# Output rows in step order, the verdict inside the order, QT moves on two queues, other homes for the raw weights

## The chip, the core and the metric

The kernel runs on one core of a Trainium2 chip. The metric is the device time of one execution in microseconds (us). TensorE is called PE, VectorE DVE, ScalarE ACT, GpSimd POOL and SyncE SP, as the profile calls them. SP and POOL each have a queue from which they issue DMA transfers in order.

## The reference

A gated linear recurrence over the sequence is followed by a two-layer network with a squared ReLU. There are B=4 batches, H=8 heads, S=768 steps, D=48 channels per head; 3072 tokens, a model width of 384 and a hidden width of 2048. q, k, v and the complex gate a are float32; the two weights w_in (384x2048) and w_out (2048x384) arrive as 64-bit floats.

```python
mag = np.sqrt(a_re * a_re + a_im * a_im)
scale = np.minimum(mag, 0.999) / (mag + 1e-06)
a_re_n, a_im_n = (a_re * scale, a_im * scale)
for t in range(S):
    ar, ai = (a_re_n[:, :, t, :, None], a_im_n[:, :, t, :, None])
    kv = np.einsum('bhd,bhe->bhde', k[:, :, t], v[:, :, t])
    S_re, S_im = (ar * S_re - ai * S_im + kv, ar * S_im + ai * S_re)
    y[:, :, t] = np.einsum('bhd,bhde->bhe', q[:, :, t], S_re)
x = y.transpose(0, 2, 1, 3).reshape(B * S, H * D)
h = np.maximum(x @ w_in, 0.0)
out = (h * h) @ w_out
```

## The kernel before

`fast_path` cuts the 3072 tokens into six units n = 0 to 5 of 512 tokens. For each unit it records the following steps.

- `load(n)` brings a, q and k into `aq` (SP, L814) and v into `vv[n % 2]` (POOL, 16 transfers, L828). A partition holds four consecutive steps.
- `chain(n)` normalises the gate, forms running products within each group of four steps (`inner`, L888 to L894), inverts them (L901 to L913), turns the totals through PE (L946), scans them on DVE and turns them back (L1092, L1097); the products with q and k follow (L1134 to L1150), and `gather` (L1181) moves the K tiles with POOL.
- `pairs(n)` takes the four head pairs in turn. `turn_pe` (units 0 and 1, on PE and ACT) or `turn` (units 2 to 5) makes the QT tile. `turn` transposes 32x32 blocks on DVE (L1217), and 12 moves (b = 0 to 3, j = 0 to 2, L1221) on SP place them. `score` (L1257, masked on DVE in L1260), `keep` (L1273) and `mix` (L1303, L1307) are matmuls. ACT copies the mixed tile from PSUM to `yt` (L1313), and SP moves it into `xT` (L1320). In `yt` and `xT` the 128 tokens of a chunk stand in the order (c, t), c being the place within a group of four steps.
- `dense(n, grp)` does the network for 256 tokens: 96 matmul rows on w1 (L1342; the profile lists two rows for each call), ReLU and Square on ACT (L1370, L1371), twice 32 rows on w2 (L1382), a copy to `ot` on ACT (L1386), and the output. Because of the order (c, t), the 128 rows of a chunk go out in four transfers of 32 rows by POOL (L1391).

The weights come in 16 pieces of 768 KB as raw 64-bit words (`fetch`, L750, POOL) into tiles that are not in use yet, their raw homes; `convert` turns a piece into float32 with one ACT step (L760) and three DVE steps (L763, L765, L769). The homes of the second weight's pieces are listed in `raw2`; a fetch marked early waits only for the first gate tiles. At the end `inspect` fetches each raw piece again and `look` (L784, L786 on DVE) tests the exponents. The `verdict` reduces all tests to one flag, which each engine loads (L1460) to decide by `tc.If` (L1461) whether a slower general path has to run. The closing barrier is at L1488.

Nearly all of this is recorded with `step` and `dma` as steps of a `Plan`. Each step has an engine, an estimated length, reads, writes and a rank. `Plan.order` is a list scheduler: it takes the engine that is free first, and on it the ready step with the lowest rank. The order that it finds is the order in which each engine gets its instructions, and from then on engines and queues work strictly in that order. Real waits come from the tiles that the instructions use. The verdict is not a step: it is issued after `plan.emit()`, so its matmul (L1408) stands behind all products.

Of the kernel before, what the change touches and what calls it, by code (L numbers as in the profile page):

```python
# [480 lines left out]
class Plan:  # L481
# [8 lines left out]
        self.wrote = {}  # L490
        self.read = {}

    def add(self, eng, dur, reads, writes, fn, rank, wire=None, group=None):

        n = len(self.steps)
        deps = set()
        for k in reads:
            deps.update(self.wrote.get(k, (None, ()))[1])
        for k in writes:
            tag, last, base = self.wrote.get(k, (None, [], []))  # L500
            if group is not None and tag == group:
                deps.update(base)
                last.append(n)
            else:
                base = list(last) + self.read.get(k, [])
                deps.update(base)
                self.wrote[k] = (group, [n], base)
                self.read[k] = []
        for k in reads:
            self.read.setdefault(k, []).append(n)  # L510
        deps.discard(n)
        self.steps.append((eng, dur, sorted(deps), fn, rank, wire))
        return n
# [63 lines left out]
def fast_path(ctx, tc, q, k, v, a_re, a_im, moe_w_in, moe_w_out, out, flag):  # L577
# [97 lines left out]
    dve.memset(ypair, 0.0)  # L675
    for t in txs:
        pool.memset(t, 0.0)
    pool.memset(txs[0].rearrange("p r (m k) -> p r m k", k=8)[:, 0, :, 0], 1.0)
    pool.memset(txs[1].rearrange("p r (m k) -> p r m k", k=4)[:, 0, :, 0], 1.0)

# [5 lines left out]
    def ts2(n):  # L686
        return n / 1920.0 + 0.18
# [1 line left out]
    def ac(n):  # L689
        return n / 1200.0 + 0.18  # L690

    def step(eng, dur, reads, writes, fn, rank, wire=None, group=None):
        return plan.add(eng, dur, reads, writes, fn, rank, wire, group)

    def dma(q, reads, writes, fn, rank, size, lat=1.8, group=None):
        step("SP" if q is sp else "POOL", 0.6 if q is sp else 0.55,
# [19 lines left out]
    def two(t):  # L716
# [8 lines left out]
            )  # L725
    raw1 = [(three(t), keys) for t, keys in raw1]
    raw1.append((xT[:, 1].bitcast(U32), [("xT", 1, m) for m in range(NM)]))
    raw2 = [w2slot(3), w2slot(2), w2slot(3), w2slot(2),
            (QT[2].bitcast(U32)[:, 0:2 * PW], [("QT", 2)]),
            (vv[1].bitcast(U32), [("v", 1)]),  # L730
            (QT[0].bitcast(U32)[:, 0:2 * PW], [("QT", 0)]),
            (QT[1].bitcast(U32)[:, 0:2 * PW], [("QT", 1)])]
    raw2 = [(two(t), keys) for t, keys in raw2]

    def piece(i):
# [35 lines left out]
    def inspect(i):  # L771
        z, s = i % 2, (i // 2) % 2
        src = piece(i)[0]
        n = piece(i)[4]
        t = ff[z].bitcast(U32)[:, s * Z:(s + 1) * Z]
        keys = [("f", z, 2 * s), ("f", z, 2 * s + 1)]
        rank = (LATE, i)
        dma(pool, [("xT", (NU - 1) % 2, NM - 1)], keys,
            lambda: pool.dma_start(out=t.rearrange("p (m f) -> p m f", m=n), in_=src),
            rank, 2 * PW * 4 * C)  # L780
        hi = t.rearrange("p (n two) -> p n two", two=2)[:, :, 1]

        def look():
            dve.tensor_scalar(out=hi, in0=hi, scalar1=0x38000000, scalar2=0x78000000,  # L784
                              op0=ALU.bitwise_xor, op1=ALU.bitwise_and)
            dve.tensor_reduce(out=odd[:, i:i + 1], in_=hi, axis=AX, op=ALU.max)  # L786
        step("DVE", ts2(PW) + tt(PW), keys, keys + [("odd",)], look, rank)

# [10 lines left out]
    def load(n):  # L801
# [20 lines left out]
        for i in range(W):  # L822
            b, s = divmod(n * L + i * C, S)
            src = v[b, :, s:s + C, :].rearrange("h (t c) d -> c t h d", c=W)
            for c in range(W):
                vrank = rank if n else (CONV, 9)
                dma(pool, [("xT", n % 2, NM - 1)] if n else [("gate",)], [("v", n % 2)],
                    lambda i=i, c=c, src=src: pool.dma_start(  # L828
                        out=t[32 * c:32 * c + 32, i], in_=src[c]), vrank, 32 * 1536, 4.0,
                    group=n)  # L830

    def chain(n):
# [9 lines left out]

        def roots(z):
            f0, f1, m2, t = col[z]
            step("ACT", ac(Z), [("a", z)], key(z, 0, 1), lambda: act.activation(
                out=ff[z][:, 0:Z], in_=A[z], func=AF.Square,
                accum_out=sums[:, n, z:z + 1]), first)
            step("DVE", tt(Y), key(z, 0, 1), key(z, 2), lambda: dve.tensor_tensor(
# [15 lines left out]
        def normalise(z):  # L864
            f0, f1, _, t = col[z]
            step("ACT", ac(Y), key(z, 3), key(z, 0), lambda: act.activation(
                out=f0, in_=t, func=AF.Copy, scale=0.999), first)
            step("ACT", ac(Y), key(z, 3), key(z, 1), lambda: act.activation(
                out=f1, in_=t, func=AF.Copy, scale=-1e-6, bias=1.0), first)
            step("DVE", tt(Y), key(z, 0, 1), key(z, 0), lambda: dve.scalar_tensor_tensor(  # L870
                out=f0, in0=f0, scalar=1.0, in1=f1, op0=ALU.min, op1=ALU.mult), first)
            a2 = A[z].rearrange("p (r x) -> p r x", r=2)
            step("DVE", tt(Z), key(z, 0), [("a", z)], lambda: dve.tensor_tensor(  # L873
                out=a2, in0=a2, in1=f0.unsqueeze(1).to_broadcast([C, 2, Y]),
                op=ALU.mult), first)
            step("ACT", ac(Y), key(z, 3), [], lambda: act.activation(
                out=junk[:, 0:Y], in_=t, func=AF.Square, saturate=False,
                accum_out=sums[:, n, 2 + z:3 + z]), first)

# [76 lines left out]
        def totals(j):  # L956
# [31 lines left out]
            def scan_x():  # L988
# [18 lines left out]
                                          scalar1=2.0 ** 114, scalar2=None, op0=ALU.is_le)  # L1007
                if not ends:
                    dve.tensor_copy(out=cx, in_=x[:, :, C])
            step("DVE", 2.3, [b, ("cx",)], [("x",), ("cx",)], scan_x, rank)  # L1010

        def product(dst, xx, y, size, reads, writes):
            shape = list(xx.shape)
# [91 lines left out]
        vt = vv[n % 2]  # L1105
        for j in range(2):
            for r in range(2):
                step("ACT", ac(Y), [("qk", j)], [], lambda j=j, r=r: act.activation(
                    out=junk, in_=QK[j][:, ts(r, Y)], func=AF.Square, saturate=False,
                    accum_out=sums[:, n, 4 + 2 * j + r:5 + 2 * j + r]), rank)  # L1110
            step("ACT", ac(Y), [("v", n % 2)], [], lambda j=j: act.activation(
                out=junk, in_=vt[:, ts(j, Y)], func=AF.Square, saturate=False,
                accum_out=sums[:, n, 8 + j:9 + j]), rank)
        for j in (2, 0, 1):
# [80 lines left out]
    def pairs(n):  # L1195
# [9 lines left out]
        def turn(i):  # L1205
# [11 lines left out]
                     lambda nat=nat, dst=dst, j=j: dve.transpose(out=dst[:, j], in_=nat), rank)  # L1217
            for b in range(W):
                for j in range(NJ):
                    dma(sp, [("a", z) if i % 2 == 0 else ("qk", z)], [("QT", s)],  # L1220
                        lambda b=b, j=j, z=z, t=t, T6=T6: sp.dma_start(  # L1221
                            out=t[32 * j:32 * j + 32, b],
                            in_=T6[32 * b:32 * b + 32, i % 2, j]), rank, 65536,
                        group=(n, i))
# [70 lines left out]
        def mix(i):  # L1295
# [4 lines left out]
            def go():  # L1300
# [10 lines left out]
                 [("yp",)], go, rank)  # L1311
            y = take("yt", 2)
            step("ACT", ac(L), [("yp",)], [("yt", y)], lambda: act.copy(  # L1313
                out=yts[y][0:64 + D], in_=ypair[0:64 + D]), rank)
            for h in range(2):
                r, end = (2 * i + h) * D, (2 * i + h + 1) * D
                p = 64 * h
# [16 lines left out]
    def dense(n, grp):  # L1334
# [39 lines left out]
        for i in range(2):  # L1374
# [11 lines left out]
            step("ACT", ac(DM), [(b,)], [("ot", o)], lambda ps=ps, o=o: act.copy(  # L1386
                out=ots[o], in_=ps), (0, n))
            r = n * L + (2 * grp + i) * C
            dst = out[r:r + C, :].rearrange("(t c) e -> c t e", c=W)
            for c in range(W):  # L1390
                dma(pool, [("ot", o)], [], lambda c=c, o=o, dst=dst: pool.dma_start(  # L1391
                    out=dst[c], in_=ots[o][32 * c:32 * c + 32]), rank, 32 * DM * 4)

    def verdict():
        pool.memset(good, 1.0)
        for lo, hi, top_ in ((0, 2, 60), (2, 4, 12), (4, NS, 20)):
            dve.tensor_scalar(out=ok[:, :, lo:hi], in0=sums[:, :, lo:hi],
                              scalar1=2.0 ** top_, scalar2=None, op0=ALU.is_le)
        dve.tensor_reduce(out=good[:, 0:1], in_=ok, axis=AXY, op=ALU.min)
        dve.tensor_reduce(out=good[:, 1:2], in_=grow, axis=AXYZ, op=ALU.min)  # L1400
        dve.tensor_reduce(out=good[:, 2:3], in_=total, axis=AXY, op=ALU.min)
        dve.tensor_reduce(out=most, in_=odd, axis=AX, op=ALU.max)
        dve.tensor_scalar(out=good[:, 3:4], in0=most, scalar1=0.0, scalar2=None,
                          op0=ALU.is_equal)
        dve.tensor_reduce(out=good[:, 7:8], in_=good[:, 0:7], axis=AX, op=ALU.min)
        dve.memset(col, 1.0)
        ps = bank["tr0"][0:1, 0:1]
        pe.matmul(ps, lhsT=good[:, 7:8], rhs=col, start=True, stop=True)  # L1408
        dve.tensor_scalar(out=flag, in0=ps, scalar1=C - 0.5, scalar2=None, op0=ALU.is_lt)

    for n in range(NU):
        load(n)
# [4 lines left out]
                convert(i)  # L1417
        chain(n)
        if n == 0:
            for j in (0, 4, 5):  # L1420
                fetch(NPIECE + j)
        pairs(n)
        if n == 0:
            for j in (1, 6, 7):
                fetch(NPIECE + j, False)
            for j in (0, 1):
                convert(NPIECE + j)
            for j in (2, 3):
                fetch(NPIECE + j, False)
            for j in range(2, NPIECE):  # L1430
                convert(NPIECE + j)
        for grp in range(2):
            dense(n, grp)
    for i in range(2 * NPIECE):
        inspect(i)
    with tc.manual_schedule():
        plan.emit()
    verdict()


@with_exitstack
# [51 lines left out]
```

## Time and profile before

| | us |
|---|---|
| median of 3 runs | 749.65 (747.22 to 751.41) |
| profiled execution | 747.83 |
| its span, first to last instruction | 746.1 |
| busy: PE, DVE, ACT, POOL | 655.4, 510.8, 347.0, 209.9 |
| end of the last product on PE | 730.8 |

The page splits the span into 40 slices of 18.65 us; each digit is the busy share of a slice in tenths. A line of waits reads: engine, operation and line, what ended the wait, total us, times, longest us. A row of stretches reads: the stretch, its length, the busy us of PE, PE's weight loads, DVE, ACT and POOL with the instruction counts in brackets, then the granted clock of PE, the share of the DMA engines and GB/s. An engine's name with a q (SPq, POOLq, PEldq) is its sequencer.

### The profile page before, as it was taken

The page shows a single profiled execution, that of the slowest core. Times are in us where ns is not written, and L with a number is a line of the kernel's source. Part 1 is how long each engine was busy: PE and PEld are TensorE (multiplying, and loading weights), DVE is VectorE, ACT ScalarE, POOL GpSimd, SP SyncE. Part 2 cuts the span into 40 slices and gives each one's busy share as a digit, 9 for nine tenths or more (in the row PEclk, how much of TensorE's full clock was granted, in tenths as well). Part 3 has the DMA queues.
Part 4 walks back from the last instruction along what each step waited for, and adds up shares of the span by engine and source line. Part 5 has one row for each costly group of instructions (what it writes and reads, how often), then busy time and mean ns, then how long its engine had stood idle before and what let it go on. Part 6 is the DMA issues. An engine that isn't in the chain of part 4 may idle for free.

```text
span 746.1 us, 10395 instructions
## 1 busy us (share of the span) xinstructions
PE 655.4 (88%) x3566; PEld 502.6 (67%) x3566; DVE 510.8 (68%) x1022; ACT 347.0 (47%) x589; POOL 209.9 (28%) x405
## 2 busy tenths in 40 slices
PE   0016988999989999999999999999999999999991
PEld 0005876587868688678698686787586787786860
DVE  4999999998796895296895287892387892354000
ACT  6763566373677422479231469331576331050400
POOL 5414460433332142240162060260110150431111
PEclk9999999899999999999999999999999999999997
DMA  8821494111721036730056730054600064794000
GB/s 286 291 98 46 120 214 173 30 36 34 215 69 24 11 93 151 208 70 0 12 126 148 179 89 1 22 135 121 201 11 9 15 147 101 220 342 174 11 11 16
DMA packets 57725, 79.44 MB, mean 106 GB/s; under 512 B 12096, under 2 KB 39360, under 8 KB 57664
## 3 DMA queue, kind: packets, MB, share of 16 engines
q1 hardware_dynamic: 40768, 37.58, 19.7%
q0 software_dynamic: 16896, 41.12, 18.5%
q8 instruction: 30, 0.49, 0.3%
q14 instruction: 31, 0.25, 0.1%
HBM read 48.76 MB, written 4.72 MB: 72 GB/s over the span
## 4 chain that ended last, share of the span: by engine, by line
PE 66%; DVE 14%; SPq 8%; DMA 4%; issue 2%; ACT 2%; POOL 0%; DVEq 0%; POOLq 0%; ACTq 0%
PE d L1382 28%; PE d L1342 27%; SPq L1221 5%; PE sc L1257 3%; DVE f L888 3%; PE tr L1273 2%; PE yp L1303 2%; PE tr L946 1%; PE yp L1307 1%; SPq L1320 1%; DMA QT<-aq 1%; SPq L814 1%; DMA xT<-yt 1%; DMA aq<-in_k_dram 1%; DVE aq L873 1%
## 5 line engine op out<-in xcount | busy, mean ns | idle before, releaser
L1382 PE MATMUL d<-w,g 128*128 128x384 f32 x768 | 261.8, 494 | 5.1 <-DVE w L769 5.1
L1342 PE MATMUL d<-xT,w 128*128 128x256 f32 x1152 | 256.4, 381 | 5.6 <-DMA xT<-yt 3.6
L1342 PEld LDWEIGHTS d<-xT,w 128*128 128x128 f32 x1152 | 218.4, 191 | 39.1 <-issue 7.2
L1382 PEld LDWEIGHTS d<-w,g 128*128 128x128 f32 x768 | 143.9, 192 | 98.0 <-DVE w L769 6.1
L1391 POOL DMA_DIRECT2D out_dram<-ot x96 | 47.7, 504 | 314.9 <-ACT ot L1386 312.2
L1181 POOL DMA_DIRECT2D KC<-f x160 | 78.4, 498 | 103.4 <-DVE f L1150 48.6
L1370 ACT ACTIVATE g<-d 128x512 f32<-128x512 f32 x96 | 57.0, 593 | 107.0 <-PE d L1342 106.7
L828 POOL DMA_DIRECT2D v<-in_v_dram x96 | 55.9, 590 | 70.4 <-PE yp L1307 26.9
L1260 DVE TENSOR_TENSOR A<-sc,mask 128x512 f32<-128x512 f32 x48 | 32.1, 683 | 57.2 <-PE sc L1257 57.2
L1371 ACT ACTIVATE g<-g 128x512 f32<-128x512 f32 x96 | 60.6, 631 | 3.1
L1257 PE MATMUL sc<-QT 96*128 96x128 f32 x384 | 50.0, 280 | 4.6 <-DMA QT<-aq 3.5
L1257 PEld LDWEIGHTS sc<-QT 96*128 96x128 f32 x384 | 47.0, 193 | 9.4 <-issue 5.6
L1139 DVE TENSOR_TENSOR f<-aq,xn 128x384 f32<-128x384 f32 (+1 forms) x64 | 44.2, 747 | 11.9 <-ACT xn L1097 11.9
L1386 ACT COPY ot<-d 128x384 f32<-128x384 f32 x24 | 11.4, 475 | 76.4 <-PE d L1382 70.4
L1313 ACT COPY yt<-yp 112x512 f32<-112x512 f32 x24 | 14.0, 583 | 70.0 <-PE yp L1307 61.1
L1150 DVE TENSOR_TENSOR f<-aq 128x384 f32<-128x384 f32 (+1 forms) x64 | 44.8, 751 | 0.5
L946 PE MATMUL tr<-perm,xn 128*128 128x128 f32 x36 | 6.4, 311 | 37.3 <-ACT xn L919 37.3
L888 DVE TENSOR_TENSOR f<-aq 128x384 f32<-128x384 f32 x72 | 36.9, 553 | 0.8
L1303 PE MATMUL yp<-A,v 128*48 128x128 f32 x384 | 36.2, 277 | 0.2
L946 PEld LDWEIGHTS tr<-perm,xn 128*128 128x128 f32 x36 | 5.0, 162 | 39.4 <-issue 29.5
L1273 PEld LDWEIGHTS tr<-v,KC 128*96 128x96 f32 x320 | 29.5, 165 | 2.3 <-issue 1.3
L1273 PE MATMUL tr<-v,KC 128*96 128x48 f32 x320 | 29.7, 246 | 0.3 <-DMA KC<-f 0.2
(153 smaller groups left out, 764.0 us busy)
## 6 DMA issues: line engine op xcount, KB each, us to landing
QT<-aq SPq DMA_DIRECT2D x192, 64.0 KB, 2.0
f<-in_moe_w_in_dram POOLq DMA_DIRECT2D x8, 768.0 KB, 7.5
f<-in_moe_w_out_dram POOLq DMA_DIRECT2D x8, 768.0 KB, 7.1
KC<-f POOLq DMA_DIRECT2D x104, 48.0 KB, 2.2
v<-in_v_dram POOLq DMA_DIRECT2D x96, 48.0 KB, 2.2
out_dram<-ot POOLq DMA_DIRECT2D x96, 48.0 KB, 1.8
xT<-yt SPq DMA_DIRECT2D x36, 96.0 KB, 2.6
aq<-in_a_re_dram SPq DMA_DIRECT2D x8, 384.0 KB, 4.2
```

The source lines that it names most:

```text
L828: lambda i=i, c=c, src=src: pool.dma_start(out=t[32 * c:32 * c + 32, i], in_=src[c]), vrank, 32 * 1536, 4.0,
L888: dve.tensor_tensor(out=f, in0=a[:, :, :, c - 1], in1=a[:, j, :, c].unsqueeze(1).to_broadcast([C, 2, HH, D]), op=ALU.mult)
L1150: lambda j=j, r=r, o=o: dve.tensor_tensor(out=o[:, :, :, r * D:(r + 1) * D], in0=qk[:, j], in1=a[:, r], op=ALU.mult), rank)
L1181: lambda i=i, c=c, queue=queue: queue.dma_start(out=kc[32 * c:32 * c + 32, i], in_=nat[32 * i:32 * i + 32, c]),
L1257: pe.matmul(sa[:, j], lhsT=T[:, j, 1, h], rhs=T[:, j, 0, h], start=True, stop=True)
L1273: pe.matmul(ps[:, j, h], lhsT=kc[:, j, (2 * i + h) % HH], rhs=v5[:, j, 2 * i + h], start=True, stop=True)
L1303: pe.matmul(ypair[64 * h:64 * h + D, ts(j, C)], lhsT=v5[:, j, 2 * i + h], rhs=aa[h][:, j], start=True, stop=at[j] is None)
L1342: pe.matmul(ps, lhsT=w1[:, f // FP, m, ts(f % FP, C)], rhs=xT[:, n % 2, m, ts(grp, G)], start=(m == 0), stop=(m == NM - 1))
L1370: act.activation(out=o, in_=ps, func=AF.Relu)
L1371: act.activation(out=o, in_=o, func=AF.Square)
L1382: pe.matmul(ps, lhsT=gt[:, f % 2, ts(i, C)], rhs=w2[:, f], start=(f == 0), stop=(f == NF - 1))
L1391: dma(pool, [("ot", o)], [], lambda c=c, o=o, dst=dst: pool.dma_start(out=dst[c], in_=ots[o][32 * c:32 * c + 32]), rank, 32 * DM * 4)
```

## The change

- The copy from PSUM to `yt` writes the tokens in step order, with steps of four elements. So the 128 rows of a chunk are contiguous in `out`, and one transfer takes the place of four. The last two chunks of unit 5 (second group) go out through SP, all others through POOL.
- `verdict` is recorded as three steps: the collecting on DVE with the rank (LATE, 99), after all steps that `check` recorded; the matmul and the flag with the rank (0, 99). The two memsets that it needs move to the start on POOL.
- Of the 12 QT moves of `turn`, the three with b = 3 go through POOL.
- `raw2` has other homes: pieces 0 and 5 in the w2 slot 3, 1 and 6 in QT[2], 2 and 7 in vv[1], 3 and 4 in QT[0] and QT[1]. Pieces 0, 1 and 2 are fetched early, and pieces 5 to 7 go into the homes of 0 to 2 after these are converted. The v loads get other ranks.

The scheduler orders everything anew. On DVE the eight conversions of the second weight stand together, ahead of most of unit 1's `inner`. On PE unit 0's first products on w2 (32 calls) stand together; in each later unit fewer products lie between the steps of `pairs`, and the verdict's matmul stands after 26 of the last 32 calls on w2 of unit 5's first group. On POOL the first v load stands ahead of the last two pieces of the first weight, and the eight last fetches of `inspect` stand together ahead of four output transfers.

```diff
-    def add(self, eng, dur, reads, writes, fn, rank, wire=None, group=None):
+    def add(self, eng, dur, reads, writes, fn, rank, wire=None, group=None, after=()):
-        deps = set()
+        deps = set(after)
...
+    def check(*args, **kw):
+        checked.append(step(*args, **kw))
...
-    raw2 = [w2slot(3), w2slot(2), w2slot(3), w2slot(2),
-            (QT[2].bitcast(U32)[:, 0:2 * PW], [("QT", 2)]),
-            (vv[1].bitcast(U32), [("v", 1)]),
+    q2, v1 = (QT[2].bitcast(U32)[:, 0:2 * PW], [("QT", 2)]), (vv[1].bitcast(U32), [("v", 1)])
+    raw2 = [w2slot(3), q2, v1,
             (QT[0].bitcast(U32)[:, 0:2 * PW], [("QT", 0)]),
-            (QT[1].bitcast(U32)[:, 0:2 * PW], [("QT", 1)])]
+            (QT[1].bitcast(U32)[:, 0:2 * PW], [("QT", 1)]),
+            w2slot(3), q2, v1]
...
-                vrank = rank if n else (CONV, 9)
+                vrank = (CHAIN, 1) if n == 1 else (DENSE, 6 + n)
...
-                    dma(sp, [("a", z) if i % 2 == 0 else ("qk", z)], [("QT", s)],
-                        lambda b=b, j=j, z=z, t=t, T6=T6: sp.dma_start(
+                    queue = pool if b == W - 1 else sp
+                    dma(queue, [("a", z) if i % 2 == 0 else ("qk", z)], [("QT", s)],
+                        lambda b=b, j=j, z=z, t=t, T6=T6, queue=queue: queue.dma_start(
...
-                out=yts[y][0:64 + D], in_=ypair[0:64 + D]), rank)
+                out=yts[y][0:64 + D].rearrange("p (j t c) -> p j c t", j=W, c=W),
+                in_=ypair[0:64 + D].rearrange("p (j c t) -> p j c t", j=W, c=W)), rank)
...
-            dst = out[r:r + C, :].rearrange("(t c) e -> c t e", c=W)
-            for c in range(W):
-                dma(pool, [("ot", o)], [], lambda c=c, o=o, dst=dst: pool.dma_start(
-                    out=dst[c], in_=ots[o][32 * c:32 * c + 32]), rank, 32 * DM * 4)
+            queue = sp if n == NU - 1 and grp == 1 else pool
+            dma(queue, [("ot", o)], [], lambda r=r, o=o, queue=queue: queue.dma_start(
+                out=out[r:r + C, :], in_=ots[o]), rank, C * DM * 4)
...
+        step("DVE", 2.2, [], [("good",)], collect, (LATE, 99), after=checked)
+        step("PE", 0.3, [("good",)], [("tr0",)], lambda: pe.matmul(
+            ps, lhsT=good[:, 7:8], rhs=col, start=True, stop=True), (0, 99))
+        step("DVE", 0.2, [("tr0",)], [("flag",)], lambda: dve.tensor_scalar(
+            out=flag, in0=ps, scalar1=C - 0.5, scalar2=None, op0=ALU.is_lt), (0, 99))
...
     for i in range(2 * NPIECE):
         inspect(i)
+    verdict()
     with tc.manual_schedule():
         plan.emit()
-    verdict()
```

More of the change, by code (lines that the diff above doesn't have):

```diff
@@ L677, in fast_path @@
         pool.memset(t, 0.0)
+    pool.memset(good, 1.0)
+    pool.memset(col, 1.0)
     pool.memset(txs[0].rearrange("p r (m k) -> p r m k", k=8)[:, 0, :, 0], 1.0)
@@ L690, in ac, with step @@
         return n / 1200.0 + 0.18
-    def step(eng, dur, reads, writes, fn, rank, wire=None, group=None):
-        return plan.add(eng, dur, reads, writes, fn, rank, wire, group)
+    checked = []
+    def step(eng, dur, reads, writes, fn, rank, wire=None, group=None, after=()):
+        return plan.add(eng, dur, reads, writes, fn, rank, wire, group, after)
+    def check(*args, **kw):
+        checked.append(step(*args, **kw))
     def dma(q, reads, writes, fn, rank, size, lat=1.8, group=None):
@@ L786, in look @@
             dve.tensor_reduce(out=odd[:, i:i + 1], in_=hi, axis=AX, op=ALU.max)
-        step("DVE", ts2(PW) + tt(PW), keys, keys + [("odd",)], look, rank)
+        check("DVE", ts2(PW) + tt(PW), keys, keys + [("odd",)], look, rank)
     def parts(n):
@@ L844, in roots @@
             f0, f1, m2, t = col[z]
-            step("ACT", ac(Z), [("a", z)], key(z, 0, 1), lambda: act.activation(
+            check("ACT", ac(Z), [("a", z)], key(z, 0, 1), lambda: act.activation(
                 out=ff[z][:, 0:Z], in_=A[z], func=AF.Square,
@@ L875, in normalise @@
                 op=ALU.mult), first)
-            step("ACT", ac(Y), key(z, 3), [], lambda: act.activation(
+            check("ACT", ac(Y), key(z, 3), [], lambda: act.activation(
                 out=junk[:, 0:Y], in_=t, func=AF.Square, saturate=False,
@@ L1009, in scan_x @@
                     dve.tensor_copy(out=cx, in_=x[:, :, C])
-            step("DVE", 2.3, [b, ("cx",)], [("x",), ("cx",)], scan_x, rank)
+            check("DVE", 2.3, [b, ("cx",)], [("x",), ("cx",)], scan_x, rank)
         def product(dst, xx, y, size, reads, writes):
@@ L1107, in chain @@
             for r in range(2):
-                step("ACT", ac(Y), [("qk", j)], [], lambda j=j, r=r: act.activation(
+                check("ACT", ac(Y), [("qk", j)], [], lambda j=j, r=r: act.activation(
                     out=junk, in_=QK[j][:, ts(r, Y)], func=AF.Square, saturate=False,
                     accum_out=sums[:, n, 4 + 2 * j + r:5 + 2 * j + r]), rank)
-            step("ACT", ac(Y), [("v", n % 2)], [], lambda j=j: act.activation(
+            check("ACT", ac(Y), [("v", n % 2)], [], lambda j=j: act.activation(
                 out=junk, in_=vt[:, ts(j, Y)], func=AF.Square, saturate=False,
@@ L1394, in verdict @@
     def verdict():
[L1395 to L1406, printed above, removed]
-        ps = bank["tr0"][0:1, 0:1]
-        pe.matmul(ps, lhsT=good[:, 7:8], rhs=col, start=True, stop=True)
-        dve.tensor_scalar(out=flag, in0=ps, scalar1=C - 0.5, scalar2=None, op0=ALU.is_lt)
+        def collect():
+            for lo, hi, top_ in ((0, 2, 60), (2, 4, 12), (4, NS, 20)):
+                dve.tensor_scalar(out=ok[:, :, lo:hi], in0=sums[:, :, lo:hi],
+                                  scalar1=2.0 ** top_, scalar2=None, op0=ALU.is_le)
+            dve.tensor_reduce(out=good[:, 0:1], in_=ok, axis=AXY, op=ALU.min)
+            dve.tensor_reduce(out=good[:, 1:2], in_=grow, axis=AXYZ, op=ALU.min)
+            dve.tensor_reduce(out=good[:, 2:3], in_=total, axis=AXY, op=ALU.min)
+            dve.tensor_reduce(out=most, in_=odd, axis=AX, op=ALU.max)
+            dve.tensor_scalar(out=good[:, 3:4], in0=most, scalar1=0.0, scalar2=None,
+                              op0=ALU.is_equal)
+            dve.tensor_reduce(out=good[:, 7:8], in_=good[:, 0:7], axis=AX, op=ALU.min)
@@ L1419, in fast_path @@
         if n == 0:
-            for j in (0, 4, 5):
+            for j in (0, 1, 2):
                 fetch(NPIECE + j)
@@ L1423, in fast_path @@
         if n == 0:
-            for j in (1, 6, 7):
+            for j in (3, 4):
                 fetch(NPIECE + j, False)
-            for j in (0, 1):
+            for j in range(NPIECE):
                 convert(NPIECE + j)
[L1428 to L1431, printed above, removed]
+                if j < 3:
+                    fetch(NPIECE + 5 + j, False)
         for grp in range(2):
```

## The prediction

> **What bounds the kernel now.** First the forty slices: TensorE (PE) is near 9 from slice 5 to the end, so after 95.9 us any gain has to come out of PE's few idle microseconds or out of what lies after its last matmul. Then PE's waits from 95 to 731 us, which list that idle time, and the clock in chosen stretches, which shows what a wait costs beyond itself.
>
> ```profile
> PE   0016988999989999999999999999999999999991
> PE d L1382 <- DVE w L769: 5.1, 2, 3.8
> PE d L1342 <- DMA xT<-yt: 3.6, 1, 3.6
> PE sc L1257 <- DMA QT<-aq: 3.5, 6, 1.4
> PE d L1342 <- issue: 1.9, 1, 1.9
> ```
>
> The 5.1 us are waits for the second weight (at 121.8 and 128.5 us), the 3.6 us the wait for unit 1's xT (219.9 to 223.5), the 3.5 us six waits for QT in units 2 to 5. Next the clock, with the granted PEclk ahead of the DMA share in each line:
>
> ```profile
> 132.00:138.00 6.00, 5.73 (x11) 3.20 (x12) 5.69 (x9) 1.53 (x3) 0.00 (x0) 0.50 0.01 3
> 223.50:226.00 2.50, 2.44 (x6) 2.02 (x7) 2.40 (x7) 0.00 (x0) 2.50 (x5) 0.50 0.41 92
> 515.00:530.00 15.00, 13.00 (x76) 9.13 (x75) 2.77 (x4) 1.74 (x2) 0.00 (x0) 0.91 0.53 138
> ```
>
> After each of the longer waits PE runs at half clock for 2.5 to 6 us: the second-weight waits cost 5.1 us and about 3 more.
>
> Last the end. PE's last product ends at 730.8, yet the span ends at 746.1. The line views of the If (L1461) and of the closing barrier (L1488), columns being duration min/median/max in ns and first and last start, show who is late:
>
> ```profile
> L1461 PEldq COMPARE_BRANCH  x1: 3862/3862/3862, 731.8 to 731.8; - x1
> L1461 SPq COMPARE_BRANCH  x1: 50/50/50, 732.0 to 732.0; - x1
> L1461 POOLq COMPARE_BRANCH  x1: 50/50/50, 733.6 to 733.6; - x1
> L1461 SPq EVENT_SEMAPHORE  x8: 17/17/17, 734.9 to 735.5; - x8
> L1461 POOLq EVENT_SEMAPHORE  x5: 17/43/43, 736.3 to 736.7; - x5
> L1461 POOLq INC_SWDGE_SEM  x1: 1716/1716/1716, 736.8 to 736.8; - x1
> L1488 POOLq DRAIN  x3: 103/188/6269, 738.5 to 745.7; - x3
> L1488 SPq DRAIN  x3: 7/7/13, 739.2 to 745.1; - x3
> L1488 PEldq DRAIN  x2: 8/8/8, 735.9 to 745.1; - x2
> ```
>
> GpSimd (POOL) issues the last four output transfers (4 x 0.49 us from 731.62), branches at 733.6, takes 2.7 us to the next block, 0.5 for its waits, 1.7 for INC_SWDGE_SEM and 6.3 for a DRAIN that ends at 744.8. PE is there at 735.9 and SyncE (SP) at 739.2; both then wait for GpSimd.
>
> **The tail (verdict in the order, last rows on SP).** The flag no longer hangs on a matmul behind the last product: the verdict matmul stands after 26 of 32 products of unit 5's first group, on before's times 689.45 - 6 x 0.645 = 685.6 us. GpSimd's last transfer is then that of 690.3 us (the two of unit 5's second group go to SP), so its branch, INC_SWDGE_SEM and DRAIN (11.2 us together) run from about 691 to 703, beside 28 us of products. SP does the end instead: ot ends at 731.3, one 192 KB transfer is issued by 732.1 (an SP issue is 0.59), 2.9 us after its branch it is in the next block (735.0), 0.6 us of waits, 0.8 us to its DRAIN as before: 736.4. GpSimd's closing 1.3 us (744.8 to 746.1) follows: 737.7, a gain of **8.4 us**. SP's transfer, landing 2.0 us (QT) to 4.2 us (the 384 KB a_re loads) after issue, is there at 734.1 to 736.3, so it costs 0 to 0.7. If the long DRAIN still runs last, the end is 736.4 + 6.3 + 1.3 = 744.0 and the gain 2.1. I take 8.4, because the DRAIN is on GpSimd alone (the others' take 7 to 17 ns) and starts when GpSimd arrives, 2.6 us after PE; bounds 2.1 and 9.
>
> The Trainium skill ("VectorE: DVE Perf Modes", The DRAIN you can't avoid) has the drains of the closing block at a constant 12 ns on all five engines. The trace agrees for four engines and not for GpSimd; by the page the 6.3 us would not be a drain to hide and the gain would be 2.1, by the row it is 8.4, and the row decides.
>
> The matmul in mid-stream adds a wait: PE's products queue behind it until DVE's looks at the weights are in. In before they end at 690.0, 4.4 us later than 685.6, but the last two fetches stood behind an output transfer that waited 9.7 us; now all eight stand ahead of the transfers. From the look that freed their buffers (ending at 674.7 for the last) a fetch lands in 4.6 and a look takes 1.5, so the looks end by 681, and about 1 us of collecting follows: 0, bound +4.4.
>
> **Raw word homes.** The second weight's pieces 0 to 2 now land early in three homes, so all eight conversions (0.56 + 0.96 + 0.96 us, 2.46 each) run on DVE back to back from 114.6: 117.1, 119.5 and so on, piece 7 at 136.1, one group of unit 1's inner products (1.68) among them. Refetches into freed homes go at 117.4 to 122.3 and take 4.7 (this stretch's row) to 9, in time. PE's 64 matmul rows of the first products then run from 119.0 without a wait to 139.7; before they ended at 151.55 with 3.5 us of other work among them: **8.4 us** gained there.
>
> It is given back. The rest of unit 1's inner products move behind the conversions: DVE is done with them at 144.6, not 129.6 (the last conversion fell at 144.6 then; the sum is the same), and ACT's Square (1.48) and the copies behind it are no longer hidden. Following ACT's order, with a Relu and Square pair (1.15) between its steps: e is copied by 157.5 where DVE wanted it at 153.1 (+4.4). ACT then has no pair between the two L1092 copies and PE no product ahead of the turned tiles, so L1139 starts at 173.4, not 172.0 (+1.4); DVE waited 2.3 and 2.0 us at 197 and 201, the second for PE products that are now done, so at 204 the lag is about 0. Unit 1's last mix then ends near 217.6 (218.9 before), but L1313 stands behind L876 now (+1.0) and is dearer (next paragraph), so xT lands near 225.2, not 223.5. Four more L1342 products (1.7 us) are done by then. Net **0**, with -4 (part of the 8.4 is kept) to +4 (the lag stays).
>
> **Rows in step order.** The yt copy (24 of them) writes with steps of 16 bytes. The nearest rows: L1092, a copy with 64-byte steps, and L963, one without.
>
> ```profile
> L963 ACT COPY e<-tr x12: 468/479/498, 38.0 to 568.5; 128x384 f32<-128x384 f32 x12
> L1092 ACT COPY f<-e x12: 829/861/872, 55.4 to 584.3; 128x384 f32<-128x384 f32 x12
> ```
>
> At L1092's rate 512 elements take 1.15 us, 0.56 over the present 0.586; at L1243's (runs of 32, 0.58 us) nothing more. I take +0.56: at xT(1) it is on the path and counted above; elsewhere ACT is 47% busy and PE has products left (0). The skill ("SBUF — State Buffer", Door 1) says that accesses within a 16-byte line run at full rate and each new line costs; 16-byte steps never reuse a line, so by it the copy is dear, and by L1243's row it is free, 0.56 us apart. GpSimd issues 22 transfers (0.72 to 0.77 us each, by the 768 KB rows) for 96 (0.498): 31 us less, of which the QT moves take back 24; off the path, since it is 28% busy.
>
> **QT on two queues.** 48 of 192 moves (0.588 each on SP) go to GpSimd (0.5, landing 2.2 like KC<-f instead of 2.0). A tile needs 9 x 0.588 = 5.3 us of SP instead of 7.1. GpSimd reaches them after 12 or 16 gathers (6 to 8 us), of which about 3.8 us pass before the first transposed half is ready, so SP stays the slower. 1.8 us earlier covers each of the six waits (largest 1.43), plus about 1.5 us of half clock after that one: up to 5 us. As the order of PE's products moves too, I take **-2**, bounds -5 and 0.
>
> **Order moved.** PE's order of products changes in every unit; the present order leaves 4.5 us of idle in units 2 to 5. I add **+0.5**, bounds 0 and +4.
>
> **Sum.** -8.4 + 0 - 2 + 0.5 = -9.9: the profiled execution's 747.83 (span 746.1, 1.7 around it) becomes 738. The runs' median is 749.65, 1.8 higher, which gives 739.8; I say 739.
>
> **Rivals.**
> *The DRAIN isn't hidden* (the change doesn't free the end): -2.1 - 2 + 0.5, 744 to 746. For it: nothing shows what the DRAIN waits for; against: all others had arrived by 739.2. Chance 0.14.
> *GpSimd's queue holds QT* (slower): in units 2 to 5 the quarter of each tile stands behind gathers and output transfers on one in-order queue, and these transfers wait for ACT up to 31 us at a time. A tile that comes late stalls scores, with nothing hiding it once PE's products in between are spent. 16 tiles: from 0.85 us per tile (13.7 us in all) it outweighs the rest by 0.5%; at 1.2 us, 753 to 755. Against: transfers stand behind products placed ahead of the scores. Chance 0.08.
> *The 8.4 us are kept as well*, if DVE's chain follows PE: 731. Against: the wait for xT shows that DVE's chain is what is late. Chance 0.08.
>
> **Numbers.** Forecast 0.70. The range 734 to 748 takes in the bounds of the start and of QT and the first rival; outside lie the second and most of the third. A measurement here tells 0.5% (3.75 us) from no change. Faster by more: forecast, third rival and a few of the first's, 0.79; within: 0.12; slower: 0.09.
>
> **What would show it.** Right: GpSimd's INC_SWDGE_SEM and long DRAIN near 700, span end 6 to 8 us after PE's last product; no wait of the second products for w; a longer one for xT near 220; yt copies near 1.1 us; QT waits below 3.5. Wrong: a 6 us DRAIN after 735, waits of PE for QT above 5 us, or xT(1) later than 230.

## The result, and the profile after

The changed kernel takes 756.57 us (median of 4 runs, 754.91 to 758.5) and the kernel before 748.43 (4 runs): ratio 1.0108, interval [1.006, 1.0155], 4 to 12 us slower where 10 us faster was forecast. The profiled execution took 758.5 us, with a span of 756.7; the last product ends at 750.4 (before: 730.8). So the end gained 9 us, and 19.6 us were lost ahead of it. PE's slices of the page of the changed kernel:

```profile
PE   0016989999888999899989999999999899999996
```

The 1 of the last slice has become a 6: the end is full. Of the 8s behind slice 10, those of slices 11, 13, 17, 21 and 32 are new. PE's waits over the whole span of the changed kernel (cause, total us, times, longest us):

```profile
PE sc L1265 <- DMA QT<-aq: 9.5, 8, 2.4
PE d L1351 <- DMA xT<-yt: 7.3, 2, 6.9
...
PE tr L1281 <- ACT QT L1251: 2.7, 2, 2.1
...
PE d L1391 <- DVE w L776: 1.2, 2, 1.0
```

L1265, L1351 and L1391 are before's L1257, L1342 and L1382. The waits for the second weight fell from 5.1 to 1.2 us as forecast; that for xT(1) rose from 3.6 to 6.9, and those for QT from 3.5 to 9.5. Here are two stretches of the changed kernel, the granted clock standing behind the five busy times:

```profile
132.00:138.00 6.00, 5.42 (x17) 3.11 (x18) 5.72 (x10) 0.00 (x0) 0.00 (x0) 1.00 0.01 3
...
586.00:598.00 12.00, 8.18 (x50) 7.15 (x52) 1.38 (x2) 1.34 (x3) 0.00 (x0) 0.72 0.80 226
```

The first, at half clock before, is at full clock. In the second, two QT waits of 2.3 and 2.4 us in unit 5 take 4.7 us, and the clock of 0.72 costs, by an estimate from its row, some 2 us more in slow matmuls (8.18 busy us x 0.28). Over the whole span, of the 19.6 us, 9.6 are more idle time of PE (75.4 to 85.0 by its end) and 10.0 are more busy time for the same 3566 instructions. Some 3 of the 19.6 us are lost ahead of 100 us, by a pace of PE that varies (last section).

The end itself, by the lines of the If (L1470) and of the closing barrier (L1497) in the changed kernel, with min/median/max ns and first and last start:

```profile
L1470 POOLq COMPARE_BRANCH  x1: 50/50/50, 710.4 to 710.4; - x1
L1470 POOLq INC_SWDGE_SEM  x1: 1336/1336/1336, 713.7 to 713.7; - x1
L1470 SPq COMPARE_BRANCH  x1: 50/50/50, 751.3 to 751.3; - x1
L1497 POOLq DRAIN  x3: 46/245/4717, 715.0 to 756.4; - x3
L1497 SPq DRAIN  x3: 7/7/13, 755.3 to 755.6; - x3
```

GpSimd's long DRAIN (4.7 us) starts at 715.0, beside 35 us of products, and SP is last: 6.3 us from the last product to the end of the span, 15.3 before.

**Where the middle went.** Between 130 and 600 us the largest new wait is for QT, so the next view is SP's queue where QT moves are issued. Unit 3 in the changed kernel, rows of the timeline with start and length in us:

```profile
368.73 12.86 SPq L1229 DMA_DIRECT2D QT<-aq  x18
381.68 1.41 SPq L821 DMA_DIRECT2D aq<-in_a_re_dram  x2
383.15 1.32 SPq L821 DMA_DIRECT2D aq<-in_a_im_dram  x2
384.56 1.39 SPq L821 DMA_DIRECT2D aq<-in_q_dram  x2
385.99 1.30 SPq L821 DMA_DIRECT2D aq<-in_k_dram  x2
387.40 3.76 SPq L1229 DMA_DIRECT2D QT<-aq  x5
```

The same place in the kernel before:

```profile
379.08 15.76 SPq L1221 DMA_DIRECT2D QT<-aq  x24
394.94 1.35 SPq L814 DMA_DIRECT2D aq<-in_a_re_dram  x2
396.40 3.10 SPq L1221 DMA_DIRECT2D QT<-aq  x5
```

Before, two of the next unit's loads stood in front of tile 2's moves, and the other six for `aq[0]` came after the unit's last move (from 415). Now all eight (5.7 us of SP and 1.5 MB) stand in front. They came there by the scheduler: it counts SP as busy for 9 moves a tile instead of 12, sees a gap after tile 1's moves and puts the ready loads into it. SP's moves behind them are issued 5.7 us later, and GpSimd's, issued from 385.7 to 389.7 while the loads fill the DMA engines (0.90 busy from 380 to 400 us), land late. In the window from 386 to 405 us of the changed kernel, the list of DMA issues (KB each, median us to landing) has

```profile
QT<-aq POOLq DMA_DIRECT2D x6, 64.0 KB, 6.3
```

where the forecast took 2.2.

The loads are not the whole of it. Of the 9.5 us of waits for QT, 4.8 lie in units 2 to 4 and 4.7 in unit 5, the last one, where no loads of a next unit are left. What came in front of unit 5's moves is on GpSimd: the first four fetches of `inspect`, 768 KB each. In the kernel before they follow when SP has issued the last QT move (at 634.1):

```profile
635.90 3.08 POOL L779 DMA_DIRECT2D f<-in_moe_w_in_dram  x4
```

In the changed kernel they are issued when SP begins the last 15 of unit 5's moves, as rows of GpSimd's and of SP's timeline show (SP issues the other 6 until 594.0):

```profile
578.50 3.03 POOL L786 DMA_DIRECT2D f<-in_moe_w_in_dram  x4
```

```profile
578.39 7.43 SPq L1229 DMA_DIRECT2D QT<-aq  x9
```

In the list of DMA issues from 578 to 592 us SP's moves take 6.8 us to land; over the whole kernel before they took 2.0:

```profile
QT<-aq SPq DMA_DIRECT2D x13, 64.0 KB, 6.8
```

### The profile page after: what moved, and what is told of

Read it like the earlier page. It is cut to its first block, busy times and chain, and to the rows that moved or that the text cites. A ratio compares the mean times of both kernels' runs of the same rounds, so it can differ in the third digit from the quotient of the medians.

```text
span 756.7 us, 10348 instructions
## 1 busy us (share of the span) xinstructions
PE 665.4 (88%) x3566; PEld 512.0 (68%) x3566; DVE 510.0 (67%) x1021; ACT 358.0 (47%) x589; POOL 197.6 (26%) x380
## 3 DMA queue, kind: packets, MB, share of 16 engines
q0 software_dynamic: 16768, 43.87, 19.6%
## 4 chain that ended last, share of the span: by engine, by line
PE 62%; DMA 5%; SPq 2%; DVE 1%; issue 1%; ACT 1%; DVEq 0%; ACTq 0%
PE d L1351 27%; PE d L1391 26%; DMA QT<-aq 4%; PE sc L1265 4%; PE tr L1281 2%; SPq L1229 1%; PE yp L1311 1%; PE yp L1315 1%; PE tr L953 1%; DMA aq<-in_q_dram 1%; SPq L1329 0%; DVE f L895 0%; DMA xT<-yt 0%; SPq L821 0%; ACT yt L1321 0%
## 5 line engine op out<-in xcount | busy, mean ns | idle before, releaser
L1351 PE MATMUL d<-xT,w 128*128 128x256 f32 x1152 | 260.9, 385 | 10.1 <-DMA xT<-yt 7.3
L1391 PE MATMUL d<-w,g 128*128 128x384 f32 x768 | 254.8, 487 | 1.2 <-DVE w L776 1.2
L1351 PEld LDWEIGHTS d<-xT,w 128*128 128x128 f32 x1152 | 220.4, 193 | 43.2 <-issue 11.4
L1391 PEld LDWEIGHTS d<-w,g 128*128 128x128 f32 x768 | 143.6, 190 | 96.1 <-DVE w L776 3.8
L1399 POOL DMA_DIRECT2D out_dram<-ot x22 | 12.3, 558 | 275.4 <-ACT ot L1395 275.4
L1265 PE MATMUL sc<-QT 96*128 96x128 f32 x384 | 57.3, 304 | 12.1 <-DMA QT<-aq 9.5
L1265 PEld LDWEIGHTS sc<-QT 96*128 96x128 f32 x384 | 51.7, 212 | 16.6 <-issue 12.5
L1268 DVE TENSOR_TENSOR A<-sc,mask 128x512 f32<-128x512 f32 x48 | 32.0, 683 | 25.5 <-PE sc L1265 25.4
L1321 ACT COPY yt<-yp 112x512 f32<-112x512 f32 x24 | 26.1, 1087 | 39.5 <-PE yp L1315 38.8
L1281 PEld LDWEIGHTS tr<-v,KC 128*96 128x96 f32 x320 | 31.3, 175 | 5.1 <-ACT QT L1251 3.2
L1281 PE MATMUL tr<-v,KC 128*96 128x48 f32 x320 | 31.9, 257 | 2.7 <-ACT QT L1251 2.7
```

The costliest lines, as they stand in the source:

```text
L1265: pe.matmul(sa[:, j], lhsT=T[:, j, 1, h], rhs=T[:, j, 0, h], start=True, stop=True)
L1281: pe.matmul(ps[:, j, h], lhsT=kc[:, j, (2 * i + h) % HH], rhs=v5[:, j, 2 * i + h], start=True, stop=True)
L1351: pe.matmul(ps, lhsT=w1[:, f // FP, m, ts(f % FP, C)], rhs=xT[:, n % 2, m, ts(grp, G)], start=(m == 0), stop=(m == NM - 1))
L1391: pe.matmul(ps, lhsT=gt[:, f % 2, ts(i, C)], rhs=w2[:, f], start=(f == 0), stop=(f == NF - 1))
```

## The experiments

Ratios are to the kernel before, with 95% intervals; 0.01 is 7.5 us. Line numbers are the changed kernel's unless said otherwise.

**1. The end alone, and one part beside it.** The first kernel is before with the edits of the verdict and of SP's last rows; the next three add the rows in step order, the raw homes with the v ranks, or QT's quarter on POOL.

```diff
+    verdict()
     with tc.manual_schedule():
         plan.emit()
-    verdict()
...
+            queue = sp if n == NU - 1 and grp == 1 else pool
```

> The kernel before with the end of the change alone: the verdict as three steps of the order, the two memsets at the start, and the last group's rows (still four transfers of 32 rows for each chunk) on SP. PE's order of products is that of before except for the verdict's matmul, after 24 of the products. Theory 1 (the end is a gain by itself and the whole loss lies ahead of it): the changed kernel's span ends 6.3 us after PE's last product and the one before ended 15.3 us after; here SP has eight issues instead of two, 6 x 0.59 = 3.5 us more, of which about half lies before the last copy. So 7 to 9 us less than before, ratio 0.988 to 0.991, last product near 731. Rival (the verdict in mid-stream holds the products): the last product moves to 735 or later and the ratio is 0.994 or more. Rival (the gain at the end is seen only because the products end later): the long DRAIN ends after the last product and the ratio is 0.997 or more.

> As the kernel with the end alone, and the rows in step order too: the strided copy to yt (1.08 us for 0.59) and one output transfer for four. PE's order of products is the same as with the end alone. Theory 1 (the copy is off the path except at unit 1's xT): 0 to +1 us against the end alone. Rival (24 dearer copies are on the path, each delaying xT or the bank of the mixed tile): up to 24 x 0.5 = 12 us more, at least +4.

> As the kernel with the end alone, and the other raw homes and v ranks too. PE's order differs from before only up to unit 2. Theory 1 (the eight conversions in front of unit 1's chain delay it by more than the products gain): xT(1) lands at 229 to 231 instead of 223.5, and the time is 2 to 4 us above the end alone. Rival (the prediction's 0: what was lost between 67 and 100 us in the changed kernel, 3 to 4 us, was a chance of the clock): within 1 us of the end alone, with xT(1) near 226.

> As the kernel with the end alone, and a quarter of the QT moves on POOL too. The scheduler then counts QT as earlier, and PE has fewer products between the steps of the pairs in units 2 to 5 (mostly none between a tile's scores and the tile before). Theory 1 (this part is where units 2 to 5 lose): PE waits for QT 8 to 11 us in place of 3.5, each wait followed by half clock, and the time is 8 to 14 us above the end alone. Rival (the prediction's step, two queues make QT earlier): 0 to 5 us below the end alone, QT waits below 3.5 us.

| kernel | median, us | ratio |
|---|---|---|
| end alone | 742.4 | 0.9907 [0.9883, 0.9932] |
| end and rows | 740.63 | 0.9883 [0.986, 0.9906] |
| end and homes | 743.9 | 0.9931 [0.9913, 0.9949] |
| end and QT's quarter | 748.93 | 0.999 [0.9963, 1.0017] |

The end is a gain by itself of 7 us, and the closing 7.1 us behind the last product of its trace leave no 6 us DRAIN there. The last product ends at 735.5, as the first rival had it, but not because of the verdict's matmul: no wait is listed around it, and 2.8 of the 4.7 us are there already at xT(1) (226.4 for 223.6). The dearer copy, together with the saved transfers, costs nothing that can be told; so the rival of 24 copies on the path is out. The homes lie 1.8 us by the ratios above the end alone, with intervals that overlap; xT(1) is there at 228.9, between the two forecasts. QT's quarter costs 6 us and is the only part that clearly loses. But its trace has only 3.2 us of waits for QT at L1265 and 1.7 at L1281 (`keep`), so theory 1's "8 to 11 us" was wrong for this kernel, and the four parts add up to about 749, not 756.6. What QT's quarter does depends on what the rest of the order is. The traces show one such difference: with QT's quarter beside the end alone the four fetches of `inspect` are issued at 607.2, behind unit 5's last QT moves (594.1). From 581 to 594 us SP's moves land after 2.0 us, unit 5 has 0.3 us of waits for QT instead of 4.7, and the stretch that was at a clock of 0.72 is at full clock:

```profile
586.00:598.00 12.00, 11.75 (x83) 8.70 (x82) 3.41 (x7) 0.58 (x1) 0.00 (x0) 1.00 0.36 86
```

**2. Queue or order.** Four edits of the changed kernel. The first puts all moves on SP. The second and third separate what the scheduler is told from which engine issues:

```diff
 # planned on two queues, issued on SP
-                        lambda b=b, j=j, z=z, t=t, T6=T6, queue=queue: queue.dma_start(
+                        lambda b=b, j=j, z=z, t=t, T6=T6, queue=sp: queue.dma_start(
 # planned on SP, issued on two queues
-                    dma(queue, [("a", z) if i % 2 == 0 else ("qk", z)], [("QT", s)],
+                    dma(sp, [("a", z) if i % 2 == 0 else ("qk", z)], [("QT", s)],
```

In the fourth the loads of a unit depend, in the order only, on the last QT moves of the unit before:

```diff
                             queue.dma_start(out=t[p0:p0 + m, j], in_=src), rank, m * 3072, 4.0 if n else 1.8,
-                            group=n)
+                            group=n, after=moved[-9:])
```

> The changed kernel with all QT moves back on SP; the end, the rows in step order and the raw homes stay. If the parts add up as measured one by one (the end 6.6 us less, the rows about -2, the homes about +1.5), 740 to 743, ratio near 0.991, and QT's quarter costs the changed kernel some 14 us instead of the 6.5 that it cost beside the end alone. If instead homes and rows together lose something of their own, 746 or more.

> The changed kernel; the scheduler still counts the moves with b = 3 on POOL, so PE's order is that of the changed kernel to the instruction, but they are issued by SP (12 x 0.59 = 7.1 us of SP per tile). Theory A (the order loses: pairs without products between them, and the next unit's loads in front of the moves of tiles 2 and 3): the wait for QT stays at 9 us or more and grows with the 1.8 us per tile that SP now needs, 755 to 765. Theory B (the moves on POOL are late): waits for QT fall below 6 us and the time to 744 to 748.

> The changed kernel; the scheduler counts all moves on SP, so PE's order is that of the changed kernel with all QT moves on SP, but the moves with b = 3 are issued by POOL. Theory A: the time is that of the kernel with all moves on SP or up to 4 us below (QT earlier by 1.8 us per tile), with waits for QT below 3 us. Theory B: it stays 8 us or more above it, with waits for QT of 8 us or more.

> The changed kernel, but a unit's loads of a, q and k wait in the order for the last QT moves of the unit before. The pairs stay as packed as they are (a or no product between most steps). Theory A in its narrower form (the loads, 2.5 to 5.6 us of SP's queue and 1.5 MB of traffic, stand in front of the moves of tiles 2 and 3): waits for QT fall from 9.5 to below 5 us, the time to 746 to 750. Theory A in its other form (the packed pairs lose, whatever the loads do): within 2 us of the changed kernel. A price that can appear in either case is that the next unit's chain starts later.

| kernel | median, us | ratio | waits for QT at the scores, us |
|---|---|---|---|
| changed kernel | 756.57 | 1.0108 [1.006, 1.0155] | 9.5 |
| all moves on SP | 742.68 | 0.9933 [0.9908, 0.9959] | 3.3 |
| planned on two, issued on SP | 776.15 | 1.0376 [1.0349, 1.0404] | 25.4 |
| planned on SP, issued on two | 739.25 | 0.9851 [0.9807, 0.9894] | none |
| loads behind the moves | 746.38 | 0.995 [0.9926, 0.9974] | 5.7 |

Theory A holds and B falls: GpSimd as the second queue is a help. With the order for one queue it takes every wait for QT away; under the order for two queues it saves 20 us against SP alone. What loses is the order. Between the changed kernel and the fourth row, which have the same work on the same engines and queues and differ in order alone, lie 17 us by the medians and 19 by the ratios (1.0108 to 0.9851). Keeping the loads back takes 10 of them away and leaves 7. That these 7 are the price of the packed pairs (pairs with few or no products between them) is not shown. In units 2 to 4, with as few products between the pairs as in the changed kernel, it waits 1.0 us for QT; the other 4.7 of its 5.7 us lie in unit 5, where the four fetches of `inspect` are again in front of the last moves (issued from 611 to 614, the moves until 626). Its time lies in the 746 to 750 of the narrower form of theory A, its waits a little above the 5 us. The 776 was beyond the 755 to 765 expected. Of its 14 waits for QT the longest, 6.3 us, is in unit 5 too, with the four fetches in front (586.5 to 589.9); the others were not followed further.

The same list of DMA issues in the fourth row's kernel, from 399 to 417 us, after two loads instead of eight:

```profile
QT<-aq POOLq DMA_DIRECT2D x7, 64.0 KB, 3.0
```

**3. The loads by themselves, and the best of the parts.** The first kernel has before's homes, planned on SP and issued on two queues. The second takes the fourth row above and moves eight (in units 2 and 4: four) loads on SP, after the scheduler is done, to where the changed kernel has them:

```diff
     def emit(self):
-        for n in self.order():
+        order = self.order()
+        for at, loads in self.front:
+            order = [n for n in order if n not in loads]
+            p = order.index(at) + 1
+            order[p:p] = loads
+        for n in order:
             self.steps[n][3]()
```

> The changed kernel with the raw homes and v ranks of before, and with the scheduler counting all QT moves on SP while POOL issues those with b = 3. PE's order is then that of before except for the verdict's matmul. If the parts add up (the end 6.6 us less, the rows about 2, the moves on POOL 3.4 us less as between the two kernels that differ by them alone), 736 to 738, ratio 0.983 to 0.986. If the homes help once QT is no longer waited for, it is no better than the 739.25 of the kernel with the new homes.

> The kernel that plans all moves on SP and issues a quarter on POOL (739.25, no wait for QT), its order on PE, DVE, ACT and POOL untouched; on SP alone the next unit's loads for aq[0] are put directly behind the moves of tile 1, where the changed kernel has them, in units 2 to 4. Theory (the loads in front of the moves of tiles 2 and 3 are what makes QT late): waits of PE for QT come back, 4 us or more, and the time is 4 to 10 us above. Rival (the products that this order leaves between the pairs cover the delay; only packed pairs lose): at most 1 us of waits, time within 1.5 us.

> The kernel before once more. In its first trace PE reached full pace at 68 us, in every kernel with a part of the change only at about 77, with the same instructions and the same waits up to there, and 3 to 4 us were lost by it. If that comes from the change (two memsets earlier on POOL), this trace shows full pace at 68 again; if it is a chance of each execution, it can show either, and 77 settles it.

> The changed kernel once more. If its waits for QT are the order's, they come back at the same tiles (2 and 3 of units 2 to 5), 8 to 11 us in all; if they were a disturbance of one execution, they are below 5.

The loads in front cost some 11 us by themselves: ratio 0.9998 [0.997, 1.0027] for 0.9851 (medians 751.11 and 739.25 us), and the waits for QT are back in a kernel that had none:

```profile
PE sc L1278 <- DMA QT<-aq: 5.9, 8, 1.9
```

Its timeline of SP in unit 3:

```profile
396.08 1.91 SPq L830 DMA_DIRECT2D aq<-in_a_re_dram  x2
398.05 1.31 SPq L830 DMA_DIRECT2D aq<-in_a_im_dram  x2
399.46 4.24 SPq L830 DMA_DIRECT2D aq<-in_q_dram  x2
403.75 1.30 SPq L830 DMA_DIRECT2D aq<-in_k_dram  x2
405.16 3.11 SPq L1240 DMA_DIRECT2D QT<-aq  x5
```

Tile 2's moves start 9.1 us after the first load. The two loads of q hold the queue for 4.2 us, 1.4 in the changed kernel; a wait for tile 1's moves, which still read `aq[0]`, is likely, and the experiment may price the loads a little high. Its runs spread from 743 to 755; the trace (span 746.6, for 737.5) shows 9.1 us: 5.9 of waits for QT, 1.3 for xT, and 1.9 of more busy time.

So the loads are some 10 to 12 of the order's 17 to 19 us: adding them alone costs 11, taking them away gives 10. The other 7 are only read from traces. In unit 5 of the changed kernel the waits behind the four fetches (4.7 us) and the low clock after them (some 2 us) come to about as much, and QT's quarter beside the end alone, whose fetches stand behind the moves, costs 6.5 us where it costs the changed kernel 13.9 (742.68 to 756.57). No run moves the fetches alone, so that share, and what the packed pairs add to it by leaving late moves uncovered, stays open.

The best of the parts is faster than both kernels: **733.77 us** (733.25 to 736.72), ratio **0.9785** [0.9762, 0.9807], 16 us below before and 2 to 4 below what the parts were expected to add up to. From its list of PE's waits, those at the places in question:

```profile
PE d L1351 <- DMA xT<-yt: 3.8, 1, 3.8
PE d L1391 <- DVE w L776: 3.4, 1, 3.4
...
PE sc L1265 <- DMA QT<-aq: 0.2, 1, 0.2
```

It lies 5 us below the same kernel with the new homes (0.9851), in another set of runs; the homes don't help there either.

The repeats: before's second trace (744.8 us span) again shows full pace at 68 us. The changed kernel's second trace (753.0) has QT waits of 9.6 us, again 8 times: they belong to the order. On the pace, see the last section.

## Why the prediction was wrong

- **Order moved, +0.5, bounds 0 and +4: the step that failed.** Its size is 17 to 19 us. The price was read off the idle time that the order of before leaves (4.5 us), as if a new order could only rearrange this. The text named PE's order alone. On the queues two things moved that were not priced: loads on SP (in unit 3, six of the eight) from behind the unit's QT moves to between tiles 1 and 2, some 10 to 12 us, and four fetches of `inspect` on GpSimd from behind unit 5's QT moves to ahead of the last of them, by the traces most of the other 7. An SP issue (0.59 us) and the size of the transfers were there to price them with. With few products left between the pairs, QT that came late became idle time and half clock. The parts as measured by the medians, the end -6.6, the rows -1.8, the homes +1.5, the second queue -3.4 and the order +17.3, add up to +7.0; the whole change measured +8.1.
- **QT on two queues, -2, bounds -5 and 0: right as a queue, in the wrong place in the sum.** Under the order for one queue it gains 3.4 us by the medians (742.68 to 739.25) and, with before's homes, 6.9 (740.63 to 733.77, in two sets of runs), and takes away nearly all the waits, as the 1.8 us per tile said. But the change tells the scheduler of the second queue by the same edit, and so it got the loss of the order with the gain of the queue.
- **The tail, -8.4: right, a little large.** 9.0 us in the trace, 7 in time for the end alone. GpSimd's DRAIN ran at 715, hidden, so the first rival is out; and the constant 12 ns that the Trainium skill has for a drain ("VectorE: DVE Perf Modes", The DRAIN you can't avoid) again doesn't hold for GpSimd (4,717 ns). That mattered: by the constant there would have been nothing to hide.
- **Verdict wait, 0: right.** DVE branches at 664.4, and no wait is listed.
- **Raw homes, 0, bounds -4 and +4: direction of both halves right, their balance somewhat off.** The second weight's waits went, and xT(1) came later. In the two traces with early pace and all moves on SP, xT(1) was there at 223.6 (before) and 226.1 (changed kernel without QT's quarter; 225.2 was forecast). In time the homes cost 1.8 us beside the end alone and 5 in the best kernel.
- **yt copy, 1.15 us for 0.59, nothing on the path but at xT(1): right.** It takes 1.08:

```profile
L1321 ACT COPY yt<-yp x24: 1056/1082/1125, 78.6 to 605.2; 112x512 f32<-112x512 f32 x24
```

and 24 of them, beside the saved transfers, cost nothing that the end and rows show (0.9883 to 0.9907). Here the Trainium skill's rule of 16-byte lines ("SBUF — State Buffer", Door 1) pointed the right way, and the row with runs of 32 elements did not.
- **The rival "GpSimd's queue holds QT"** came near the right time by luck, not by its mechanism, and its sum is off: 1.2 us for each of 16 tiles are 19.2 on the forecast's 739.8, which makes 759 and not 753 to 755. GpSimd's moves do come late (6.3 us to land), but with two loads in front instead of eight they take 3.0, and taking them off GpSimd made the time worse (776).

## What to carry to other kernels

An edit to what a list scheduler is told is two edits: the resource, and the order that follows from it. Price them apart, by planning with the old figures and issuing on the new queue, and keep the order that has slack where transfers are late. When an order moves, look at every queue and not at the busiest engine alone: large loads that slip in front of small moves on their queue cost more here than the second queue gained, and large fetches on the other queue went with moves that took 6.8 us to land instead of 2.0.

## What was not expected of the hardware

PE's pace after its first long idle time varies between executions with the same instructions and waits. From 66 to 77 us, the changed kernel:

```profile
66.00:77.00 11.00, 10.33 (x57) 9.58 (x57) 8.30 (x19) 2.87 (x6) 4.86 (x10) 1.00 0.44 108
```

and the kernel before:

```profile
66.00:77.00 11.00, 10.33 (x109) 9.62 (x107) 10.30 (x24) 3.79 (x7) 6.09 (x13) 1.00 0.39 100
```

The same 10.33 busy us hold 57 matmuls in one and 109 in the other, at a granted clock of 1.00 in both; the slow pace lets xT(1) land about 3 us later (226.4 with the end alone, 223.6 before). Both traces of before had the early pace and both of the changed kernel the late one (57 and 63 matmuls). But the kernel planned on two queues and issued on SP, which differs from the changed kernel only in who issues QT moves from unit 2 on, had the early one:

```profile
66.00:77.00 11.00, 10.33 (x110) 9.64 (x108) 10.36 (x24) 4.31 (x7) 6.17 (x13) 1.00 0.41 105
```

So did the kernels without QT's quarter (112), with the loads behind the moves (108) and with the best of the parts (108). So some 3 us of the first comparison of traces are not to be put down to the change. What decides between the two paces stays open, and so does how many of the runs behind each median had which. From single traces a difference of 3 us ahead of 100 us is not to be read as an effect.
